# RWKV-7 recurrence on one core: the carry turned feature-major, head pairs issued in turn on row and column halves

## The chip, the core and the metric

One core of one Trainium2 chip runs the whole program. The metric is device time in microseconds. Before the change three runs gave 2215.01, 2234.22 and 2242.56 us, so the median is 2234.22 us. TensorE (PE) does the matrix products and writes its results to PSUM; VectorE (DVE), ScalarE (ACT) and GpSimd (POOL) do the element-wise work; SyncE (SP) issues loads.

## What is computed

For 4 batches and 8 heads of dimension 40, a state matrix is carried over 768 steps. Its output, rearranged to 4 x 768 x 320, then goes through a low-rank token mixer and a channel MLP:

```python
for t in range(S):
    y[:, :, t] = np.einsum('bhd,bhde->bhe', rt, state)
    Sa = np.einsum('bhde,bhe->bhd', state, at)
    state_decay = state * wt[:, :, None, :] - np.einsum('bhd,bhe->bhde', Sa, bt)
    state = state_decay + np.einsum('bhd,bhe->bhde', vt, kt)
...
h = xt @ U @ V
u = x + h.transpose(0, 2, 1)
ch = np.maximum(u @ w_ch1, 0.0) @ w_ch2
return (u + ch).astype(np.float32)
```

## The kernel before, in words

The program has two parts. Part 1 is the recurrence, in 24 units; a unit is one chunk of 128 steps of one batch, with its 8 heads as 4 pairs. Unit n is chunk n // 4 of batch n % 4, so the state of a batch is needed again four units later. Part 2 (the mixer and the MLP) follows and is not touched by the change.

A unit passes through three stages in three successive iterations of the loop at line 403. `prep` transposes the six inputs so that features lie on the partitions (head 0 of a pair from partition 0, head 1 from partition 64), forms the running product of w (`GT`, a scan) and its reciprocal (`ip`), scales A by the one and B and K by the other, and transposes K, B and the running product back (`tk`, `tb`, `tp`). `solve` runs once for each slot, that is for the four heads at one end of the pairs: it makes the scores `pf`, `pe` and `pc` from matmuls over 40 rows, and then inverts a 128 x 128 triangular matrix for each head by doubling blocks. Level 0 is a transpose; at each of the six further levels PE makes `px`, DVE turns it into `g`, PE makes `pt` and `pu`, ACT copies them to `tm` and `tt`, and POOL masks the next `fl` (lines 283 to 315). `carry` also runs once for each slot: it makes the right side `pr`, the solution `pX` with steps on the partitions and once more as `pXf` with features on the partitions, the new state `ps`, the product `pg`, the output `py` and the turned state `pS`. Its matmuls are mostly 40 columns wide.

A loop iteration takes `prep` of unit n, `solve` of unit n - 1 and `carry` of unit n - 2 in turn, one step of each at a time, until each is used up (line 412). A scheduler then fixes the order on each engine from this order, the dependencies and the free buffers. All PSUM tiles come from one pool of 8 banks. Each engine takes its own instructions strictly in that order.

The weights of part 2 arrive as 64-bit floats in 26 pieces (`raw`), one asked for in each iteration. DVE converts each with nine instructions at lines 132 to 144. The scheduler put all 26 in the first iterations, where they ended by 350 us.

In the profile's names `px<-tm,fl` is the instruction that writes `px` from `tm` and `fl`; 40*128 after MATMUL is rows x columns of the array in use. A float32 matmul of full precision stands in the records twice, a transpose once.

Of the kernel before, what the change touches and what calls it, by code (L numbers as in the profile page):

```python
# [12 lines left out]
outside, it redoes the recurrence step by step, which holds for any values.  # L13
"""
# [7 lines left out]
F32 = mybir.dt.float32  # L22
I32 = mybir.dt.int32
ALU = mybir.AluOpType
# [8 lines left out]
def kernel(  # L33
# [45 lines left out]
    # ML[l][t, s]: t and s in one block of 2n = 2^(l+1), s in its first half and t in its second.  # L79
# [19 lines left out]
    def weights(pool):  # L99
        """Loads part 2's weights, a piece at each step."""  # L100
# [47 lines left out]
    with ExitStack() as p1:  # L148
# [6 lines left out]
        S = st.tile([128, NB * NP, D], F32, name="S")  # L155
        ST = st.tile([128, NB * NP, D], F32, name="ST")
        # Per unit and partition: how many w are in range, and the other inputs' sums of squares.
# [34 lines left out]
        def prep(u):  # L192
            """Per unit of 8 heads: head pairs on the partitions (64 apart), steps on the free axis."""
# [51 lines left out]
            for key, t in (("k", fm["K"]), ("b", fm["B"]), ("p", gt)):  # L245
                p = psum(f"t{key}")
                for j in range(NP):
                    nc.tensor.transpose(out=p[:, j * L:(j + 1) * L], in_=t[:, j, 0:L], identity=ID[:])
                fm[key] = fmp.tile([128, NH, D], F32, name=f"t{key}", bufs=3)
                nc.scalar.activation(out=fm[key][:], func=ACTF.Copy,  # L250
                                     in_=p[:].rearrange("p (h e) -> p h e", e=DP)[:, :, 0:D])
                yield
# [5 lines left out]

        def solve(u, slot):
            """T, E and C of the 4 heads in one slot."""  # L260
            fm, q, lo = u.fm, u.q[slot], 64 * slot
            hi = lo + D

            def pairs(name, x, y):
                p = psum(name)
                for i in range(4):
                    nc.tensor.matmul(out=p[:, i * L:(i + 1) * L], lhsT=x[lo:hi, i, :],  # L267
                                     rhs=y[lo:hi, i, :], start=True, stop=True)
                return four(p)

            ft = qp.tile([128, 4, L], F32, name="ft")
            nc.scalar.activation(out=ft[:], in_=pairs("pf", fm["A"], fm["B"]), func=ACTF.Copy)
            yield
            q["E"] = qp.tile([128, 4, L], F32, name="E", bufs=3)
            nc.vector.tensor_tensor(out=q["E"][:], in0=pairs("pe", fm["K"], fm["A"]), in1=over4(MU),
                                    op=ALU.mult)
            yield
            q["C"] = qp.tile([128, 4, L], F32, name="C", bufs=3)
            nc.vector.tensor_tensor(out=q["C"][:], in0=pairs("pc", fm["V"], fm["R"]), in1=over4(MU),  # L279
                                    op=ALU.mult)  # L280
            yield
            tm = tt = None
            for l in range(NLEV):
                fl = qp.tile([128, 4, L], F32, name="fl", bufs=3)
# [9 lines left out]
                g = qp.tile([128, 4, L], F32, name="g", bufs=3)  # L294
# [23 lines left out]
        def carry(u, slot):  # L318
            """Outputs and the state at the chunk's end."""
            fm, q, lo = u.fm, u.q[slot], 64 * slot  # L320
            hi = lo + D
            first, last = u.c == 0, u.c == NCH - 1
            s0 = u.b * NP
            hs = [2 * i + slot for i in range(4)]
            s_, st_ = S[lo:hi, s0:s0 + NP, :], ST[lo:hi, s0:s0 + NP, :]

            def small(name, p0=0, p1=128):
                p = psum(name)
                return p[p0:p1, 0:4 * D].rearrange("p (i e) -> p i e", e=D)

            p = small("pr")
            for i in range(4):
                if not first:
                    nc.tensor.matmul(out=p[:, i, :], lhsT=fm["A"][lo:hi, i, :], rhs=st_[:, i, :],
                                     start=True, stop=False)
                nc.tensor.matmul(out=p[:, i, :], lhsT=q["E"][:, i, :], rhs=fm["v"][:, hs[i], 0:D],
                                 start=first, stop=True)
            rh = qp.tile([128, 4, D], F32, name="rh")
            nc.scalar.activation(out=rh[:], in_=p, func=ACTF.Copy)
            yield  # L340
            p = small("pX")
            for i in range(4):
                nc.tensor.matmul(out=p[:, i, :], lhsT=q["T"][:, i, :], rhs=rh[:, i, :],  # L343
                                 start=True, stop=True)
            nx = qp.tile([128, 4, D], F32, name="nx")
            nc.scalar.activation(out=nx[:], in_=p, func=ACTF.Copy, scale=-1.0)
            p = psum("pXf")
            for i in range(4):
                nc.tensor.matmul(out=p[lo:hi, i * L:(i + 1) * L], lhsT=rh[:, i, :], rhs=q["T"][:, i, :],
                                 start=True, stop=True)  # L350
            if u.xf is None:
                u.xf = qp.tile([128, 4, L], F32, name="xf", bufs=1)
            xf = u.xf
            nc.scalar.activation(out=xf[lo:hi], in_=four(p)[lo:hi], func=ACTF.Copy)
            yield
            if not last:
                p = small("ps", lo, hi)
                for i in range(4):
                    nc.tensor.matmul(out=p[:, i, :], lhsT=fm["k"][:, hs[i], :],
# [241 lines left out]
```

## Time and profile before

| | before |
|---|---|
| median of 3 runs | 2234.22 us (2215.01 to 2242.56) |
| span of the profiled execution | 2228.6 us |
| PE busy | 2188.2 us (98%) |
| DVE busy | 744.1 us (33%) |
| ACT busy | 488.5 us (22%) |
| POOL busy | 506.9 us (23%) |
| mean granted TensorE clock | 0.807 |

The profile covers one execution; it gives no other time for it than the span. Busy time is the time in which an engine had an instruction in work; for PE it says nothing on how full the array was. The granted clock is 1.0 where TensorE had its full 2.4 GHz and 0.5 where it had 1.2 GHz. The chain of work that ended last lies wholly on PE.

### The profile page before, as it was taken

Reading aid. Unit: us, or ns where it says so; the run is one execution under the profiler, and the core shown is the slowest. Engines: PE = TensorE matmul, PEld = TensorE weight load, DVE = VectorE, ACT = ScalarE, POOL = GpSimd, SP = SyncE. Lnnn points to the kernel's source line nnn. Section 1 sums busy time; section 2 is a strip of 40 time slices with the busy share of each in tenths; the row PEclk is TensorE's granted clock in tenths of the full one; section 3 lists DMA queues with packets and bytes.
Section 4 is the critical chain, followed back from the end, with each engine's and each line's share of the span. In section 5 each row is a group of like instructions: output and inputs, shape, how many; then the busy total and the mean of one; then the engine's idle time right before and its main releaser. Section 6 shows DMA issues by size and latency. Waiting matters only on the chain. (4 is left out here: it accounts for less than half of the span.)

```text
span 2228.6 us, 32787 instructions
## 1 busy us (share of the span) xinstructions
PE 2188.2 (98%) x13890; PEld 1921.7 (86%) x13890; DVE 744.1 (33%) x1439; ACT 488.5 (22%) x921; POOL 506.9 (23%) x453
## 2 busy tenths in 40 slices
PE   7999999999999999999999999999999999999999
PEld 6888898999999999999999999999999996565555
DVE  7666654323323323322333233233322121111111
ACT  2223221321321232132123213212321320000000
POOL 5333332322222232132223123222322320000000
PEclk8978876876886787688678678767866887999999
DMA  4111111000001001000100100000000000000000
GB/s 81 41 30 38 38 35 24 10 16 16 10 13 18 13 8 18 13 13 13 19 10 10 19 13 13 13 16 8 12 1 1 1 1 1 9 15 12 9 9 18
DMA packets 155286, 36.62 MB, mean 16 GB/s; under 512 B 150600, under 2 KB 153672, under 8 KB 155136
## 3 DMA queue, kind: packets, MB, share of 16 engines
q1 hardware_dynamic: 153216, 27.54, 6.7%
q0 software_dynamic: 1920, 6.95, 1.1%
q8 instruction: 111, 1.82, 0.3%
q14 instruction: 39, 0.32, 0.0%
HBM read 30.54 MB, written 3.93 MB: 15 GB/s over the span
## 5 line engine op out<-in xcount | busy, mean ns | idle before, releaser
L285 POOL TENSOR_TENSOR fl<-ft,ML 128x512 f32<-128x512 f32 x336 | 422.8, 1274 | 1220.7 <-PE px L291 541.2
L295 DVE TENSOR_TENSOR g<-ID,px 128x512 f32<-128x512 f32 x336 | 230.0, 687 | 494.4 <-PE px L291 487.2
L304 PE MATMUL pt<-g,tt 128*128 128x128 f32 x2304 | 311.7, 280 | 19.0 <-DVE g L295 16.7
L304 PEld LDWEIGHTS pt<-g,tt 128*128 128x128 f32 x2304 | 280.7, 193 | 27.7 <-DVE g L295 18.1
L311 PE MATMUL pu<-tt,g 128*128 128x128 f32 x1920 | 254.4, 276 | 0.0
L311 PEld LDWEIGHTS pu<-tt,g 128*128 128x128 f32 x1920 | 234.7, 193 | 0.0
L291 PE MATMUL px<-tm,fl 128*128 128x128 f32 x1920 | 234.0, 275 | 0.0
L291 PEld LDWEIGHTS px<-tm,fl 128*128 128x128 f32 x1920 | 224.0, 192 | 0.0
L307 ACT ACTIVATE tm<-pt 128x512 f32<-128x512 f32 x240 | 143.3, 597 | 218.4 <-PE pt L304 218.4
L314 ACT ACTIVATE tt<-pu 128x512 f32<-128x512 f32 x240 | 143.3, 597 | 74.9 <-PE pu L311 74.9
L543 PE MATMUL p<-uf,W 104*128 104x384 f32 (+1 forms) x480 | 156.4, 485 | 0.0
L543 PEld LDWEIGHTS p<-uf,W 104*128 104x128 f32 (+1 forms) x480 | 90.7, 189 | 63.3
L559 PE MATMUL p<-W,hid 128*128 128x320 f32 x480 | 136.1, 438 | 0.0
L559 PEld LDWEIGHTS p<-W,hid 128*128 128x128 f32 x480 | 89.0, 190 | 44.3 <-issue 10.5
L395 ACT ACTIVATE S<-pS 40x160 f32<-40x160 f32 x40 | 11.9, 299 | 499.7 <-PE pS L393 499.2
L279 DVE TENSOR_TENSOR C<-pc,MU 128x512 f32<-128x512 f32 x48 | 33.2, 692 | 239.0 <-PE pc L267 166.6
L381 PE MATMUL py<-tk,C 128*128 128x40 f32 x384 | 103.9, 364 | 0.0
L383 PE MATMUL py<-tb,ng 128*128 128x40 f32 x384 | 101.3, 358 | 0.0
L343 PEld LDWEIGHTS pX<-rh,tl 128*128 128x128 f32 x384 | 83.7, 321 | 13.8 <-issue 13.6
L548 ACT ACTIVATE hid<-p 128x384 f32<-128x384 f32 x40 | 19.6, 491 | 340.2 <-PE p L543 340.2
L371 PE MATMUL pg<-fR,xf 40*128 40x128 f32 x384 | 93.5, 431 | 0.0
L379 PE MATMUL py<-S,fR 40*128 40x40 f32 x320 | 91.9, 381 | 0.0
(138 smaller groups left out, 2832.4 us busy)
## 6 DMA issues: line engine op xcount, KB each, us to landing
nW<-in_w_dram SPq DMA_DIRECT2D x24, 160.0 KB, 2.6
nA<-in_a_dram SPq DMA_DIRECT2D x24, 160.0 KB, 2.6
nB<-in_b_dram SPq DMA_DIRECT2D x24, 160.0 KB, 2.6
nK<-in_k_dram SPq DMA_DIRECT2D x24, 160.0 KB, 2.5
nR<-in_r_dram SPq DMA_DIRECT2D x24, 160.0 KB, 2.6
nV<-in_v_dram SPq DMA_DIRECT2D x24, 160.0 KB, 2.5
out_dram<-o SPq DMA_DIRECT2D x24, 160.0 KB, 1.8
raw<-in_moe_w_ch_dram POOLq DMA_DIRECT2D x10, 320.0 KB, 3.2
```

The costliest lines, as they stand in the source:

```text
L285: nc.gpsimd.tensor_tensor(out=fl[:], in0=ft[:], in1=over4(ML[l]), op=ALU.mult)
L291: nc.tensor.matmul(out=p[:, i * L:(i + 1) * L], lhsT=fl[:, i, :], rhs=tm[:, i, :], start=True, stop=True)
L295: nc.vector.tensor_tensor(out=g[:], in0=over4(ID), in1=four(p), op=ALU.subtract)
L304: nc.tensor.matmul(out=p[:, i * L:(i + 1) * L], lhsT=tt[:, i, :], rhs=g[:, i, :], start=True, stop=True)
L307: nc.scalar.activation(out=tm[:], in_=four(p), func=ACTF.Copy)
L311: nc.tensor.matmul(out=p[:, i * L:(i + 1) * L], lhsT=g[:, i, :], rhs=tt[:, i, :], start=True, stop=True)
L314: nc.scalar.activation(out=tt[:], in_=four(p), func=ACTF.Copy)
L371: nc.tensor.matmul(out=p[:, i * L:(i + 1) * L], lhsT=xf[lo:hi, i, :], rhs=fm["R"][lo:hi, i, :], start=True, stop=True)
L381: nc.tensor.matmul(out=p[:, i, :], lhsT=q["C"][:, i, :], rhs=fm["k"][:, hs[i], :], start=first, stop=False)
L383: nc.tensor.matmul(out=p[:, i, :], lhsT=ng[:, i, :], rhs=fm["b"][:, hs[i], :], start=False, stop=True)
L543: nc.tensor.matmul(out=p[:, 0:GN], lhsT=W1[i][0:n, j * 128:(j + 1) * 128], rhs=uf[i][0:n, :], start=(i == 0), stop=(i == len(CT) - 1))
L559: nc.tensor.matmul(out=p[:, 0:DM], lhsT=hid[:, f, j * L:(j + 1) * L], rhs=W2[:, f, :], start=False, stop=(f == NJ - 1))
```

## The change

The scores of both slots are made together: for each of the three products the matmuls of the two heads of a pair are issued in turn, with head 0 on rows 0 to 63 of the array and head 1 on rows 64 to 127, into two PSUM tiles. The operands now span 64 rows with zeros beyond 40. The carry runs once for a unit, for all 8 heads, and keeps the right side, the solution and the output with features on the partitions. Its matmuls are 128 columns long (64 in the state products), and the two heads of a pair are issued in turn into column halves: head 0 writes partitions 0 to 63 and head 1 writes 64 to 127 of one PSUM tile. Where a product needs steps on the partitions, a transpose of four blocks (`flip`) turns it. In `prep` the two transposes of scaled K and B are replaced by one transpose of the reciprocal (`pi`) and two DVE products with the loaded K and B; the transpose of the running product is gone, since the output is scaled while its features lie on the partitions. The rings of `fl` and `g` have 2 buffers in place of 3. An iteration's steps are merged by a table of step counts (carry 8, prep 8, scores and inverse 17), so that a step of the carry comes after about every second step of the inverse.

```diff
+            p = psum("pi")
+            for j in range(NP):
+                nc.tensor.transpose(out=p[:, j * L:(j + 1) * L], in_=ip[:, j, :], identity=ID[:])
+            for key, t in (("k", "K"), ("b", "B")):
+                fm[key] = fmp.tile([128, NH, DP], F32, name=f"t{key}", bufs=3)
+                nc.vector.tensor_tensor(out=fm[key][:], in0=p[:].rearrange("p (h e) -> p h e", e=DP),
+                                        in1=u.nat[t][:], op=ALU.mult)
+            yield
...
+        def pairs(name, x, y):
+
+            out = [psum(f"{name}{s}") for s in range(2)]
+            for i in range(NP):
+                for s in range(2):
+                    nc.tensor.matmul(out=out[s][:, i * L:(i + 1) * L],
+                                     lhsT=x[DP * s:DP * (s + 1), i, :],
+                                     rhs=y[DP * s:DP * (s + 1), i, :], start=True, stop=True)
+            return [four(p) for p in out]
...
-                fl = qp.tile([128, 4, L], F32, name="fl", bufs=3)
+                fl = qp.tile([128, 4, L], F32, name="fl", bufs=2)
...
+        def columns(p, n, lhs, rhs, first, last):
+
+
+            for i in range(NP):
+                for s in range(2):
+                    nc.tensor.matmul(out=p[half(s), i * n:(i + 1) * n], lhsT=lhs(i, s), rhs=rhs(i, s),
+                                     start=first and i == 0, stop=last, skip_group_check=True)
+
+        def carry(u):
...
+            p = psum("pr")
+            columns(p, L, nat4(fm["v"]), score("E"), True, first)
+            if not first:
+                columns(p, L, feat(st_), feat(fm["A"]), False, True)
+            rf = qp.tile([128, NP, L], F32, name="rf", tag="xx", bufs=2)
+            nc.scalar.activation(out=rf[:], in_=four(p), func=ACTF.Copy)
+            yield
+            p = flip("prt", rf)
+            rh = qp.tile([128, NH, DP], F32, name="rh", tag="rn", bufs=1)
+            nc.vector.tensor_copy(rh[:].rearrange("p (i s) e -> p i (s e)", s=2), p)
+            yield
+            p = psum("pX")
+            columns(p, L, nat4(rh), score("T"), True, True)
...
+            for s, p in enumerate(pairs("pg", xf, fm["R"])):
+                t = qp.tile([128, NP, L], F32, name="ng")
+                nc.vector.tensor_tensor(out=t[:], in0=p, in1=over4(MUN), op=ALU.mult)
+                ng.append(t)
+            yield
+            py = psum("py")
+            columns(py, L, nat4(fm["k"]), score("C"), True, False)
+            columns(py, L, nat4(fm["b"]), lambda i, s: ng[s][:, i, :], False, first)
+            if not first:
+                columns(py, L, feat(s_), feat(fm["R"]), False, True)
...
+                columns(p, DP, nat4(fm["k"]), nat4(fm["v"]), True, False)
+                columns(p, DP, nat4(fm["b"]), nat4(nx), False, True)
...
+        def merged(*steps):
+
+            lists = [[g, 0, n] for g, n in steps]
+            while lists:
+                x = min(lists, key=lambda x: (x[1] + 0.5) / x[2])
+                if next(x[0], x) is x:
+                    lists.remove(x)
+                x[1] += 1
...
+            if n >= 2:
+                gens.append((carry(units[n - 2]), 8))
             if n < N:
-                gens.append(prep(units[n]))
+                gens.append((prep(units[n]), 8))
...
-            while gens:
-                gens = [g for g in gens if next(g, g) is not g]
+                gens.append((both(), 17))
+            merged(*gens)
```

The order on PE around the solution `pX` of one unit. Before, the pieces of the carry stand together, and one row of names holds one slot (`tl` is the finished inverse, `rh` the right side, `ps` the new state, `pg` and `py` the output's parts):

```order
L213 MATMUL pa<-ID,nA_140 128x128 x4
L267 MATMUL pe<-fA,fK 128x128 x8
L343 MATMUL pX<-rh,tl 128x40 x4
L349 MATMUL pXf<-tl,rh 40x128 x4
L343 MATMUL pX<-rh,tl 128x40 x4
L349 MATMUL pXf<-tl,rh 40x128 x4
L267 MATMUL pc<-fR,fV 128x128 x8
L359 MATMUL ps<-nV_132,tk 40x40
L361 MATMUL ps<-nx,tb 40x40
```

Now, from the scores to the second level of the inverse:

```order
L264 MATMUL pc_4889<-fR,fV 128x128
L264 MATMUL pc_4890<-fR,fV 128x128
L357 MATMUL prt<-ID,rf 128x128 x4
L213 MATMUL pa<-ID,nA_139 128x128 x4
L296 MATMUL px<-ID,fl 128x128 x8
L298 MATMUL px<-g,fl 128x128 x8
L333 MATMUL pX<-tl,rh 64x128 x8
L311 MATMUL pt<-g,tt 128x128 x4
L318 MATMUL pu<-tt,g 128x128 x4
L311 MATMUL pt<-g,tt 128x128 x4
L318 MATMUL pu<-tt,g 128x128 x4
L298 MATMUL px<-tm,fl 128x128 x8
```

The solution moved behind level 0 and the first `px` of level 1; `pXf` is gone, and `pg`, `py`, `ps` and `pS` now stand behind later levels, one at a time.

The order on DVE at the same place. Before, from the last `g` of one inverse on (`fA` is scaled A, `E` a masked score, `sink` a range test):

```order
L295 TENSOR_TENSOR g<-ID,px 128x512 x12
L224 SCALAR_TENSOR_TENSOR GT_153<-pw,zeros 128x128 x4
L197 TENSOR_SCALAR wc<-nW_147 128x8x40
L233 RECIPROCAL ip<-GT_153 128x512
L230 TENSOR_TENSOR fA<-pa,GT_153 128x512
L275 TENSOR_TENSOR E<-pe,MU 128x512 x2
L200 SCALAR_TENSOR_TENSOR sink,WOK<-nW_147,wc 128x320
```

Now:

```order
L302 TENSOR_TENSOR g<-ID,px 128x512 x4
L250 TENSOR_TENSOR tk<-pi,nK_127 128x512
L250 TENSOR_TENSOR tb<-pi,nB_143 128x512
L224 SCALAR_TENSOR_TENSOR GT_153<-pw,zeros 128x128 x4
L197 TENSOR_SCALAR wc<-nW_147 128x8x40
L233 RECIPROCAL ip<-GT_153 128x512
L278 TENSOR_TENSOR E<-pe_5405,MU 128x512
L278 TENSOR_TENSOR E<-pe_5406,MU 128x512
L282 TENSOR_TENSOR C<-pc_5419,MU 128x512
L369 COPY rh<-prt 128x512
L230 TENSOR_TENSOR fA<-pa,GT_153 128x512
L302 TENSOR_TENSOR g<-ID,px 128x512 x2
```

Before, the products of the carry (`sn`, `ng`) and the range tests also lay between the reciprocal and the next unit's first `g`, and on PE most of the carry. Now `wc`, the reciprocal and five products stand between the scan and the first `g`, and PE has only `pe`, `pc`, `prt`, `pa` and level 0 between `pw`, which the scan waits for, and the `px` of level 1, which waits for that `g`.

## Rows read from the trace of the kernel before

**Rows 1.** Stretches: us, then busy us (instructions) of PE, PEld, DVE, ACT, POOL; clock; DMA.

```profile
21.40:351.10 329.70, 310.73 (x2399) 294.92 (x2398) 215.94 (x452) 94.78 (x177) 115.45 (x105) 0.84 0.16 36
351.10:1684.60 1333.50, 1333.50 (x9134) 1242.98 (x9133) 427.87 (x800) 332.15 (x627) 340.39 (x272) 0.76 0.07 13
1684.60:1860.00 175.40, 174.74 (x1080) 161.93 (x1079) 37.57 (x57) 38.67 (x72) 39.99 (x32) 0.72 0.00 1
1860.00:2228.60 368.60, 362.08 (x1248) 214.94 (x1248) 49.44 (x92) 19.64 (x40) 0.00 (x0) 0.99 0.03 11
```

**Rows 2.** The same view: one regular unit, its inverse, most of its carry.

```profile
949.50:1028.00 78.50, 78.50 (x542) 73.17 (x541) 25.18 (x47) 19.58 (x37) 20.04 (x17) 0.76 0.08 14
949.50:987.00 37.50, 37.50 (x335) 36.38 (x334) 12.27 (x17) 17.48 (x32) 12.93 (x12) 1.00 0.03 5
987.00:1014.40 27.40, 27.40 (x142) 24.09 (x142) 9.70 (x25) 2.10 (x5) 4.64 (x5) 0.50 0.14 25
```

**Rows 3.** Timeline of PE in the inverse at 2.4 GHz: start us, us, instruction, records.

```profile
949.71 0.68 PE L393 MATMUL pS<-ID,ST 40*40 40x40 f32 x16
950.32 0.66 PE L213 MATMUL pV<-ID,nV 128*128 128x128 f32 x4
950.81 1.06 PE L304 MATMUL pt<-g,tt 128*128 128x128 f32 x8
951.70 1.06 PE L311 MATMUL pu<-tt,g 128*128 128x128 f32 x8
...
954.38 0.60 PE L213 MATMUL pR<-ID,nR 128*128 128x128 f32 x4
954.82 1.39 PE L291 MATMUL px<-tm,fl 128*128 128x128 f32 x11
```

**Rows 4.** Timeline of PE at 1.2 GHz where two scores of different row halves meet.

```profile
28.73 0.42 PE L267 MATMUL pe<-fA,fK 40*128 40x128 f32 x1
28.89 0.42 PE L267 MATMUL pc<-fR,fV 40*128 40x128 f32 x1
28.94 0.42 PE L267 MATMUL pe<-fA,fK 40*128 40x128 f32 x1
29.11 0.42 PE L267 MATMUL pc<-fR,fV 40*128 40x128 f32 x1
```

**Rows 5.** Groups by line: count, then busy us, mean ns of one, idle before.

```profile
L233 DVE RECIPROCAL ip<-GT 128x512 f32<-128x512 f32 x24 | 80.3, 3345 | 0.0
L224 DVE TENSOR_TENSOR_SCAN GT<-pw,zeros 128x128 f32<-128x128 f32 x96 | 32.8, 404 | 34.6 <-PE pw L213 34.6
L197 DVE TENSOR_SCALAR wc<-nW 128x320 f32<-128x320 f32 x24 | 9.8, 408 | 2.5 <-DMA nW<-in_w_dram 2.5
L275 DVE TENSOR_TENSOR E<-pe,MU 128x512 f32<-128x512 f32 x48 | 32.9, 689 | 41.8 <-PE pe L267 41.7
L295 DVE TENSOR_TENSOR g<-ID,px 128x512 f32<-128x512 f32 x336 | 230.0, 687 | 494.4 <-PE px L291 487.2 <-PE px L289 7.2
L285 POOL TENSOR_TENSOR fl<-ft,ML 128x512 f32<-128x512 f32 x336 | 422.8, 1274 | 1220.7 <-PE px L291 541.2 <-PE px L289 480.9 <-ACT ft L272 198.2
```

**Rows 6.** Stretches as in rows 1, where PE ran short of work early on.

```profile
103.00:106.40 3.40, 1.19 (x11) 0.95 (x10) 3.25 (x4) 0.44 (x1) 2.57 (x2) 1.00 0.29 48
106.40:109.80 3.40, 3.38 (x16) 3.38 (x17) 3.26 (x8) 0.60 (x1) 0.08 (x1) 0.50 0.02 5
109.80:113.20 3.40, 3.40 (x32) 3.40 (x32) 0.15 (x1) 2.12 (x4) 0.52 (x1) 1.00 0.28 78
```

**Rows 7.** Timeline of PE at 1.2 GHz, then (last row) at 2.4 GHz.

```profile
1011.11 1.11 PE L213 MATMUL pB<-ID,nB 128*128 128x128 f32 x4
1012.02 1.91 PE L289 MATMUL px<-ID,fl 128*128 128x128 f32 x8
...
1014.42 0.42 PE L381 MATMUL py<-tk,C 128*128 128x40 f32 x2
```

**Rows 8.** Waits: who for whom, total us, times, longest us.

```profile
DVE bits L132 <- DMA raw<-in_moe_w_ch_dram: 38.6, 21, 3.1
```

More of the change, by code (lines that the diff above doesn't have):

```diff
@@ L316, in solve @@
             q["T"] = tm
-        def carry(u, slot):
-            fm, q, lo = u.fm, u.q[slot], 64 * slot
-            hi = lo + D
-            first, last = u.c == 0, u.c == NCH - 1
[L323 to L327, printed above, removed]
-                p = psum(name)
[L329 to L339, printed above, removed]
-            yield
[L341 to L354, printed above, removed]
@@ L355, in carry @@
             yield
             if not last:
-                p = small("ps", lo, hi)
-                for i in range(4):
-                    nc.tensor.matmul(out=p[:, i, :], lhsT=fm["k"][:, hs[i], :],
-                                     rhs=fm["v"][:, hs[i], 0:D], start=True, stop=False)
-                    nc.tensor.matmul(out=p[:, i, :], lhsT=fm["b"][:, hs[i], :], rhs=nx[:, i, :],
-                                     start=False, stop=True)
-                pend = fm["g"][lo:hi, :, L:L + 1].to_broadcast([D, NP, D])
+                p = flip("pXt", xf)
@@ L364, in carry @@
                 if first:
-                    sn = p
+                    nc.vector.tensor_tensor(out=st_, in0=ps_, in1=pend, op=ALU.mult)
                 else:
-                    sn = qp.tile([128, 4, D], F32, name="sn")[lo:hi]
-                    nc.vector.tensor_tensor(out=sn, in0=p, in1=st_, op=ALU.add)
-            p = psum("pg")
-            for i in range(4):
-                nc.tensor.matmul(out=p[:, i * L:(i + 1) * L], lhsT=xf[lo:hi, i, :],
-                                 rhs=fm["R"][lo:hi, i, :], start=True, stop=True)
@@ L373, in carry @@
-            ng = qp.tile([128, 4, L], F32, name="ng")
-            nc.vector.tensor_tensor(out=ng[:], in0=four(p), in1=over4(MUN), op=ALU.mult)
-            yield
-            p = small("py")
-            for i in range(4):
-                if not first:
-                    nc.tensor.matmul(out=p[:, i, :], lhsT=fm["R"][lo:hi, i, :], rhs=s_[:, i, :],
-                                     start=True, stop=False)
-                nc.tensor.matmul(out=p[:, i, :], lhsT=q["C"][:, i, :], rhs=fm["k"][:, hs[i], :],
-                                 start=first, stop=False)
-                nc.tensor.matmul(out=p[:, i, :], lhsT=ng[:, i, :], rhs=fm["b"][:, hs[i], :],
-                                 start=False, stop=True)
@@ L385, in carry @@
-            x = XTM[:, u.b * NCH + u.c, :].rearrange("p (i s e) -> p i s e", s=2, e=D)[:, :, slot, :]
-            pt = fm["p"][:].rearrange("p (i s) e -> p i s e", s=2)[:, :, slot, :]
-            nc.vector.tensor_tensor(out=x, in0=p, in1=pt, op=ALU.mult)
-            if not last:
-                nc.vector.tensor_tensor(out=st_, in0=sn, in1=pend, op=ALU.mult)
-                yield
-                p = small("pS", lo, hi)
-                for i in range(4):
-                    nc.tensor.matmul(out=p[:, i, :], lhsT=st_[:, i, :], rhs=ID[lo:hi, lo:hi],
-                                     start=True, stop=True)
-                nc.scalar.activation(out=s_, in_=p, func=ACTF.Copy)
@@ L396, in carry @@
-            yield
+                    sn = qp.tile([128, NP, DP], F32, name="sn", tag="rn", bufs=1)
+                    nc.vector.tensor_tensor(out=sn[:], in0=ps_, in1=st_, op=ALU.add)
+                    nc.vector.tensor_tensor(out=st_, in0=sn[:], in1=pend, op=ALU.mult)
+                yield
+                p = psum("pS")
+                columns(p, DP, feat(st_), lambda i, s: ID[half(s), half(s)], True, True)
+                nc.scalar.activation(out=s_, func=ACTF.Copy,
+                                     in_=p[:, 0:NP * DP].rearrange("p (i e) -> p i e", e=DP))
@@ L404, with both @@
             gens = []
+            if n >= 2:
+                gens.append((carry(units[n - 2]), 8))
             if n < N:
-                gens.append(prep(units[n]))
+                gens.append((prep(units[n]), 8))
             if 1 <= n < N + 1:
-                gens += [solve(units[n - 1], 0), solve(units[n - 1], 1)]
-            if n >= 2:
-                gens += [carry(units[n - 2], 0), carry(units[n - 2], 1)]
-            while gens:
-                gens = [g for g in gens if next(g, g) is not g]
+                u = units[n - 1]
+                def both(u=u):
+                    yield from scores(u)
+                    g = [solve(u, 0), solve(u, 1)]
+                    while g:
+                        g = [x for x in g if next(x, x) is not x]
+                        yield
+                gens.append((both(), 17))
+            merged(*gens)
             next(wload, None)
```

82 lines of the change are left out of this document (52 added, 30 removed).

## The prediction

> **What bounds the kernel now.** I read first the stretches of the whole program, then those of one unit, then the timeline of TensorE (PE) inside it, and last the groups by line for what the other engines cost. Over the 17 units from 351 us on, PE is busy for all of 1333.5 us, 78.4 us a unit, at a mean clock of 0.76 [rows 1]. In one unit DVE is busy for 25.2 of 78.5 us, ACT for 19.6, POOL for 20.0 [rows 2]. So PE sets the pace, and the question is what it does. The inverse runs 37.5 us at 2.4 GHz; in the 27.4 us of carry and scores behind it the clock is 0.50, that is 1.2 GHz, though PE shows no gap [rows 2]. A unit is thus about half dense work at full clock and half small work at half clock. In the five units before 351 us PE lacks work for 19 us in all and DVE is busy for 216 of 330 us [rows 1], since the weights are converted there; DVE also waited 38.6 us for their pieces [rows 8]. Part 2 takes 368.6 us [rows 1] and stays.
>
> **The sum for PE, per unit, at 2.4 GHz.**
> - Inverse, unchanged: a group of four matmuls takes 0.89 us from start to start [rows 3]. 34 groups are 30.3 us. The 8 transposes of level 0, at 0.11 each (four in 0.44 [rows 3]), are 0.9 us.
> - Transposes: 28 in `prep` (36 before) and 12 in the carry (none before): 40 x 0.11 = 4.4 us.
> - Row halves: 24 scores and 8 of `pg`. Where a score of one half met one of the other, both streams kept their own rate: `pe` starts at 28.73 and 28.94, `pc` at 28.89 and 29.11, a record each 0.21 us in each stream at 1.2 GHz [rows 4]. A matmul is two records, so two halves together make two matmuls in 0.43 us, or one each 0.107 us at 2.4 GHz. 32 x 0.107 = 3.4 us. Before, heads of one half followed each other in fours, and so overlapped only at the seams.
> - Halves in both directions (state times A, state times R): the diagonal `pS` matmuls took 16 records in 0.61 us with a change of mode in it [rows 3], less than one by one at the same length. 16 x 0.107 = 1.7 us, and `pS` again 0.6.
> - Column halves over all 128 rows: 32 matmuls 128 columns long, and 16 of `ps` half as long. No row of before shows these. They are bounded by 0.107 (as the row halves) and 0.22 us (one after another, a quarter of 0.89 [rows 3]). I take 0.107, because both kinds of halves that rows show overlap. 3.4 + 0.9 = 4.3 us; by the upper bound 8.8.
> - Changes of mode: the new order has 17 a unit. The transposes behind `pS` took 0.49 us where four alone take 0.44, and the entry is part of the 0.61 [rows 3]. I take 0.1 us for each, 1.7 us.
>
> Sum: 30.3 + 0.9 + 4.4 + 3.4 + 1.7 + 0.6 + 4.3 + 1.7 = 47.3 us if the clock stays at 2.4 GHz and nothing waits. A rule of the Trainium skill speaks against the change here: "TensorEngine Tiling (Array Packing)", Key Properties, says that changing the tiling mode drains TensorE. By rows that drain is the 0.1 us above, and even 0.3 for each would leave 50.7.
>
> **What PE will wait for.** DVE takes its work in order. At the seam of two units it holds, once `pw` is there: four scans (4 x 0.40), `wc` (0.41), the reciprocal (3.35), two `E`, one `C`, `rh`, `fA` and the first `g` (6 x 0.69) [rows 5], 9.5 us in all. The products `tk` and `tb` stand before the scans and are done while `pw` is awaited. From the last `g` of a unit PE needs 1.0 us for the last `pt`, 0.9 for `pyt` and `pi`, 1.0 for `pf`, 2.0 for `pr` and 0.5 for `pw`, so `g` comes at 5.4 + 9.5 = 14.9 us. Behind `pw` PE has `pe` and `pc` (1.9), `prt` and `pa` (0.9) and level 0 (0.9), and so is through at 9.1 us. It then waits 5 to 6 us for `g`; I take 5.5. Before, the reciprocal was hidden by the long `pr`, `pX` and `pXf` at 1.2 GHz; that cover is what the change removes.
>
> Other DVE work is covered: the range tests, `ng`, `yf`, `sn` and the new state stand where PE has a group of `pt` and `pu` (3.6 us) to do first. POOL's next `fl` costs 2 x 1.27 us [rows 5] from the end of a `px`, and that buffer is wanted 4.5 us later, so two buffers suffice in place of three. ACT copies about as much as before, and its 20 us a unit [rows 2] stay far below 56. SP's loads of K and B now wait until `tk` and `tb` have read the old ones, a whole unit ahead of their use.
>
> The wait costs clock too. Where PE was busy for only 1.19 of 3.4 us, the clock was 0.50 in the next stretch, and 16 records were done there where the one behind, at 1.00, took 32 [rows 6]. I expect one such drop a unit with 4 us of PE work left in it: 2 us. Handovers as they now are around each `g` add 1 us. So a unit is 47.3 + 5.5 + 2 + 1 = 55.8; I say 56 us.
>
> **The sum for the program.** From 351 to 1685 us: 17 x (78.4 - 56) = 381 us less. The last steps, 175.4 us [rows 1]: a unit without state (54), an inverse with carry and no `prep` (44), a carry alone, eight handovers of some 2.5 us (20), so 118, or 57 less. The five early units, 330 us: DVE's 216 us grow by some 2 us a unit and by three more conversions at 4 us (now 25 in this stretch), and its waits for pieces add up to 38.6 us. That makes 240 to 280 us on DVE in order with PE's 250. I take 295, or 35 less. Part 2: nothing. 2228.6 - 381 - 57 - 35 = 1755.6 us of span. The median of the runs lies 5.6 us above the span, so **1761 us**; the handovers at the start that I can't price make me say 1765.
>
> **The rivals.**
> - Column halves run one after another: 4.5 us a unit, over 23 units 104 us, **1870 us**. Against it: the row halves; for it: no row shows it. "TensorE: Matmul & The Clock Gate", Part 3 of the Trainium skill, says that weights load beside running matmuls only where their row group differs, which column halves don't do. The trace disagrees for full-size matmuls: loads of 0.19 us each would not fit otherwise into 0.89 us for four. Chance 0.20.
> - The change doesn't do what it says: no halves overlap at all. Then row halves and diagonals cost 5.1 us more as well: 9.6 a unit, **1985 us**. Rows 4 speak against it. Chance 0.06.
> - The clock falls earlier, because transposes don't hold it up; the stretch before the wait is mostly transposes (28 of them, 3.1 us, from `pyt` to level 0). These and the first dense matmuls would run at 1.2 GHz: 3 us more a unit, 1835 us; and if the wait grew to 10 us by the longer DVE queue, **1930 us**. Part 4 of the same page of the Trainium skill says that transposes don't engage the full clock. The trace disagrees: at 1.2 GHz twelve transposes, `pB` and `px`, were followed by a `py` at 2.4 GHz [rows 7]. Chance 0.08.
> - No wait at the seam, because DVE is ahead: 5.5 + 2 us less a unit, **1600 us**. Against it is the order on DVE. Chance 0.05.
> - Slower: the small pieces, spread among the inverse, keep the clock at 1.2 GHz all through, where before the inverse had 37.5 us at 2.4 GHz in one piece. 47.3 us become 94.6, with DVE's wait then hidden: 16 us more a unit, some 23 x 16 = 370, **2600 us**. It decides once 45 us of a unit lie at 1.2 GHz, since 56 + 45/2 is 78.5. Against it: what was slow before were 40-column and 40-row pieces, and the new pieces fill rows and are 128 long. Chance 0.04.
>
> **How the numbers follow.** My forecast, 1765 us, has 0.57 with a range of its own of 1700 to 1830: 53 to 59 us a unit. The range of 1690 to 1920 adds the column halves and the milder clock case, and leaves out the other ends. Within 2% of 2234 (2190 to 2279, about what a measurement of this kernel can tell from no change) is hardly any case: 0.02. Faster 0.94, slower 0.04.
>
> **What would show it.** In the profile after: `px` and `pt` groups at 0.89 us; `pe` and `pc` 16 records in 0.9 us and the 16 matmuls of `py` in column halves in 1.7 us (3.5 if one after another); PE idle for 5 to 6 us a unit before the `px` of level 1, released by DVE's `g`, with the reciprocal in front of it; the clock at 0.93 or so in part 1. A unit of over 60 us, a clock below 0.85, or waits of PE elsewhere would make the prediction wrong.

## The result and the profile after

The changed kernel takes **1778.4 us** (median of 4 runs, 1776.1 to 1780.1) against 2227.3 us (4 runs, 2215.0 to 2242.6): a ratio of 0.799, interval 0.795 to 0.804. The prediction said 1765, range 1690 to 1920.

The changed kernel's page, cut to its span, the engines' busy time, and one group by line:

```profile
span 1778.4 us, 32076 instructions
PE 1590.9 (89%) x13586; PEld 1371.8 (77%) x13586; DVE 822.1 (46%) x1451; ACT 445.2 (25%) x777; POOL 507.5 (29%) x453
...
L298 PE MATMUL px<-g,fl 128*128 128x128 f32 x384 | 86.4, 416 | 143.9 <-DVE g L302 142.3
```

PE is no longer busy all the time, and most of its idle time in part 1 (142.3 of some 171 us) stands in front of one line: the `px` of level 1, for DVE's `g`. The stretches that answer to [rows 1] (five early units, 17 units, last steps, part 2; columns as there):

```profile
20.10:337.80 317.70, 245.99 (x2375) 231.04 (x2373) 252.04 (x469) 87.42 (x152) 116.30 (x107) 0.91 0.17 39
337.80:1299.60 961.80, 875.39 (x8927) 825.37 (x8925) 468.22 (x802) 302.83 (x525) 341.58 (x274) 0.95 0.10 18
1299.60:1412.70 113.10, 100.17 (x1001) 93.57 (x1000) 39.69 (x59) 33.01 (x57) 38.69 (x32) 0.96 0.01 1
1412.70:1778.40 365.70, 361.97 (x1248) 215.13 (x1248) 49.44 (x92) 19.61 (x40) 0.00 (x0) 0.99 0.03 11
```

A unit now takes 961.8 / 17 = 56.6 us where it took 78.4. One unit, from its `pw` to the next, and then the same unit in three pieces (same columns; it answers to [rows 2]):

```profile
904.40:961.30 56.90, 51.82 (x531) 48.84 (x529) 27.61 (x47) 17.88 (x31) 20.07 (x17) 0.94 0.11 19
904.40:912.20 7.80, 4.56 (x54) 4.01 (x52) 7.09 (x10) 0.60 (x1) 6.32 (x6) 1.00 0.23 40
912.20:919.00 6.80, 4.96 (x28) 4.77 (x30) 5.58 (x11) 0.00 (x0) 2.33 (x2) 0.50 0.14 24
919.00:961.30 42.30, 42.30 (x453) 40.06 (x449) 14.95 (x28) 17.29 (x30) 11.42 (x10) 1.00 0.08 15
```

Of 56.9 us, 5.1 are idle and 6.8 lie at 1.2 GHz, from the last 1.8 us of the idle time on; the rest is at 2.4 GHz, where before the carry's 27.4 us were at half that. The timeline of PE at this seam (start us, us, instruction, records; in brackets idle time before, and who ended it):

```profile
902.37 1.09 PE L333 MATMUL pr<-E,nV 128*64 128x128 f32 x16
903.40 1.09 PE L333 MATMUL pr<-fA,ST 64*64 64x128 f32 x16
904.42 0.66 PE L213 MATMUL pw<-ID,wc 128*128 128x128 f32 x4
905.00 1.16 PE L264 MATMUL pe<-fA,fK 64*128 64x128 f32 x16
906.00 1.06 PE L264 MATMUL pc<-fR,fV 64*128 64x128 f32 x16
...
907.92 1.04 PE L296 MATMUL px<-ID,fl 128*128 128x128 f32 x8
914.04 3.75 PE L298 MATMUL px<-g,fl 128*128 128x128 f32 x16 [5.08 <-DVE g L302]
```

And DVE at the same time:

```profile
905.11 1.37 DVE L224 TENSOR_TENSOR_SCAN GT<-pw,zeros 128x128 f32<-128x128 f32 x4 [2.44 <-PE pw L213]
906.40 0.71 DVE L197 TENSOR_SCALAR wc<-nW 128x320 f32<-128x320 f32 x1
907.03 3.34 DVE L233 RECIPROCAL ip<-GT 128x512 f32<-128x512 f32 x1
910.29 1.22 DVE L278 TENSOR_TENSOR E<-pe,MU 128x512 f32<-128x512 f32 x2
911.43 0.67 DVE L282 TENSOR_TENSOR C<-pc,MU 128x512 f32<-128x512 f32 x1
912.03 0.67 DVE L369 COPY rh<-prt 128x512 f32<-128x512 f32 x1
912.63 0.68 DVE L230 TENSOR_TENSOR fA<-pa,GT 128x512 f32<-128x512 f32 x1
913.22 1.27 DVE L302 TENSOR_TENSOR g<-ID,px 128x512 f32<-128x512 f32 x2
```

PE's level 0 was done by 909; `g` of slot 0 starts at 913.22, 8.80 us behind `pw`, because DVE works through its queue without a gap. That is the wait the prediction named, with the reciprocal in it. Column halves: the 16 records of `pr<-E,nV` take 1.03 us from start to start, one change of mode included.

### The profile page after: what moved, and what is told of

Read it like the earlier page. It is cut to its first block, busy times and chain, and to the rows that moved or that the text cites. A ratio compares the mean times of both kernels' runs of the same rounds, so it can differ in the third digit from the quotient of the medians.

```text
span 1778.4 us, 32076 instructions
## 1 busy us (share of the span) xinstructions
PE 1590.9 (89%) x13586; PEld 1371.8 (77%) x13586; DVE 822.1 (46%) x1451; ACT 445.2 (25%) x777; POOL 507.5 (29%) x453
## 5 line engine op out<-in xcount | busy, mean ns | idle before, releaser
L311 PE MATMUL pt<-g,tt 128*128 128x128 f32 x2304 | 318.8, 283 | 20.1 <-DVE g L302 19.3
L298 PE MATMUL px<-g,fl 128*128 128x128 f32 x384 | 86.4, 416 | 143.9 <-DVE g L302 142.3
L298 PEld LDWEIGHTS px<-g,fl 128*128 128x128 f32 x384 | 80.9, 321 | 149.1 <-issue 147.1
L374 ACT ACTIVATE xf<-pX 128x512 f32<-128x512 f32 x24 | 14.3, 597 | 341.8 <-PE pX L333 258.3
L583 DVE TENSOR_SCALAR hid<-p 128x384 f32<-128x384 f32 x40 | 22.3, 558 | 133.2 <-PE p L580 133.2
L233 DVE RECIPROCAL ip<-GT 128x512 f32<-128x512 f32 x24 | 80.2, 3341 | 0.0
L599 DVE TENSOR_TENSOR o<-p,XTM 128x320 f32<-128x320 f32 x24 | 11.8, 492 | 134.8 <-PE p L596 134.8
```

Source lines behind the costliest of these rows:

```text
L233: nc.vector.reciprocal(out=ip[:], in_=gt[:, :, 1:L + 1])
L298: nc.tensor.matmul(out=p[:, i * L:(i + 1) * L], lhsT=fl[:, i, :], rhs=tm[:, i, :], start=True, stop=True)
L311: nc.tensor.matmul(out=p[:, i * L:(i + 1) * L], lhsT=tt[:, i, :], rhs=g[:, i, :], start=True, stop=True)
L583: nc.vector.tensor_scalar_max(hid[:, j, :], p[:, 0:GN], 0.0)
```

## The experiments

Eleven kernels. `col_serial`, `row_serial`, `spread_alone` and `no_spread`, the first, second, fourth and fifth below, have 2 runs each, the others 4. Times are medians, and the ratio is to the kernel before, run beside it. Where no ratio stands, those runs gave no interval.

### Which halves pay

**Column halves not in turn.** In `columns`, the two loops change places, so that all heads of one half come before the other half:

```diff
-            for i in range(NP):
-                for s in range(2):
+            for s in range(2):
+                for i in range(NP):
```

> The changed kernel with the column halves issued one head after the other (four matmuls of head 0, then four of head 1) in place of in turn; nothing else differs. Theory (halves in turn overlap, halves in blocks overlap only at the seam): each block of eight 128-column matmuls grows from about 1.0 us to 1.7 to 1.8 us, four such blocks and two of half length a unit, 4.0 us a unit, 23 units: 1778 + 92 = 1870 us. Rival (the array overlaps them whatever their order, or did not overlap them before either): 1770 to 1785 us.

Measured: 1850.0 us, ratio 0.830 (0.824 to 0.837), so 71.6 us more than the change. Two groups in this kernel's timeline of PE, beside 1.03 and 1.02 us from start to start in the changed kernel:

```profile
883.68 1.58 PE L333 MATMUL pr<-E,nV 128*64 128x128 f32 x16
885.19 1.58 PE L333 MATMUL pr<-fA,ST 64*64 64x128 f32 x16
```

Each takes 1.51 us, half a microsecond more. So column halves and diagonals overlap when issued in turn, which no row of before showed, and this is worth 3.5 us a unit (its 17 units took 1021.7 us in place of 961.8; 0.25 us a unit of it is a longer wait for `g`). It is less than the 4.5 of the rival, since the end of one half still overlaps the start of the other: the records there are 0.05 us apart, where in the rest of the group they are 0.11.

**Row halves not in turn.** The same edit in `pairs` (`pf`, `pe`, `pc`, `pg`).

> The changed kernel with the row halves of the scores and of pg issued one head after the other; nothing else differs. Theory: pf, pe, pc and pg grow by 0.8 us each, but pe and pc stand before the 5 us wait of TensorE at the seam of two units and are swallowed by it; pf is ahead of pw, on which the scan waits, and counts, and so does pg: 1.6 us a unit, 1778 + 37 = 1815 us, with the wait 1.6 us shorter. Rival (the wait is not set by DVE's chain behind pw): all four count, 3.2 us a unit, 1850 us. Rival (no overlap by rows): 1778 us.

Measured: 1771.9 us, ratio 0.795 (0.789 to 0.802): no slower than the change, and under every time that was expected. `pf` and `pg` cost 0.55 us more each, and `pe` with `pc` took 2.7 instead of 2.0 us, but the wait that follows shrank. The same `px` as above, in this kernel (its `pw` starts at 837.51), and DVE beside it:

```profile
845.66 1.27 DVE L302 TENSOR_TENSOR g<-ID,px 128x512 f32<-128x512 f32 x2
846.49 3.75 PE L298 MATMUL px<-g,fl 128*128 128x128 f32 x16 [3.68 <-DVE g L302]
846.86 0.32 DVE L197 TENSOR_SCALAR wc<-nW 128x320 f32<-128x320 f32 x1
```

PE idles 3.68 us in place of 5.08, for two reasons. 0.75 us is the longer `pe` and `pc`: what PE saves ahead of a wait for DVE it spends waiting. The other 0.65 is a change that the edit did not ask for: the scheduler put the clamp `wc`, which took 0.71 us ahead of `g`, behind it, so that `g` starts 8.15 us behind `pw` instead of 8.80. This hides more than half of what `pf` and `pg` cost, so the time does not show that row halves are worth nothing. The 17 units took 967.2 us in place of 961.8, and the five early ones 305.5 in place of 317.7; in the early ones PE's waits for `g` at line 298 fell from 51.3 to 26.2 us, and the section on the prediction says what the clamp has to do with it.

**The row halves alone, in the kernel before.** The scores of both slots are issued in turn ahead of the inverse; the carry keeps its old shapes and order.

```diff
+        def scores(u):
+            fm = u.fm
+            for s, p in enumerate(pairs("pf", fm["A"], fm["B"])):
...
-                gens += [solve(units[n - 1], 0), solve(units[n - 1], 1)]
+                gens.append(both())
```

> The kernel before with only the three score matrices changed: both slots' row halves issued in turn, sixteen to a group, ahead of the inverse; the carry keeps its shapes and its order. Theory of the row halves: 24 matmuls fewer in sequence, 3.4 us a unit at 2.4 GHz, of which the changed kernel showed nothing since its TensorE waits for VectorE there; in the kernel before half of that stretch runs at 1.2 GHz, so 3 to 6 us a unit would show if TensorE is the bound there, 22 x 3 = 66 to 22 x 6 = 132 us less: 2100 to 2165. Rival, from the run with row halves serial: the wait for VectorE at the head of a unit swallows it here too: 2215 to 2235. Rival: the scores of both slots ahead of the inverse delay level 0 of slot 0 and lengthen the wait: 2240 to 2290.

Measured: 2028.4 us, ratio 0.918 (0.908 to 0.929), far below what was expected. The 17 units of this kernel:

```profile
301.30:1492.00 1190.70, 1190.70 (x9134) 1115.06 (x9133) 423.35 (x800) 330.89 (x627) 339.09 (x272) 0.84 0.08 14
```

PE is busy all through, and a unit takes 70.0 us where it took 78.4. Nearly all of that is the clock, 0.84 in place of 0.76. An estimate from these rows: 1333.5 us at 0.76 [rows 1] are some 1013 us of work at 2.4 GHz, and 1190.7 us at 0.84 some 1000. So of the 143 us that the 17 units gained, the halves' own time is no more than some 13. Whether the halves or the new order of the scores raised the clock, this run doesn't separate; the next one shows that an order alone can.

### What the spreading does

**Old shapes, new spreading.** The kernel before with its carry's steps spread by the change's rule.

> The kernel before with its carry spread among the inverse's steps by the same kind of table (carry 5 steps of both slots, prep 10, inverse 17), all shapes as they were. Theory (shapes pay): the 40-column and 40-row pieces need 60 us a unit even at 2.4 GHz and still drop the clock round pr and py: 66 to 72 us a unit, 1960 to 2090 us. Rival (spreading pays by the clock): 62 us or less a unit and a clock over 0.92: under 1880 us. Rival (spreading does nothing): 2200 to 2240 us.

Measured: 2059.6 us, ratio 0.925 (0.918 to 0.931). Its 17 units:

```profile
312.70:1528.00 1215.30, 1214.99 (x9133) 1139.16 (x9132) 459.70 (x800) 332.07 (x628) 344.70 (x272) 0.85 0.08 14
```

The old shapes run faster spread out, with PE still busy throughout. By the same estimate the work is 1033 us at 2.4 GHz, no less than the 1013 before: the gain is the clock's.

**New shapes, old order.** The steps of `prep`, scores and inverse, and carry are again taken one each in turn.

```diff
-            merged(*gens)
+            gens = [g for g, _ in gens[1:] + gens[:1]] if n >= 2 else [g for g, _ in gens]
+            while gens:
+                gens = [g for g in gens if next(g, g) is not g]
```

> The changed kernel with the old order of steps: one step of prep, of scores and inverse, and of the carry in turn until each is used up, so that the carry stands together at the unit's start. Theory (the new shapes pay, not their spreading): TensorE's work is the same 47 us, the small work now stands where DVE does its scan and reciprocal, so the wait shrinks: 1740 to 1800 us, clock at 0.93 or more. Rival (the spreading among the inverse keeps the clock up): the carry drops the clock to 1.2 GHz again for some 15 us a unit and the time is over 1850 us.

Measured: **1682.2 us**, ratio 0.755 (0.750 to 0.760). The spreading, good for the old shapes, costs the new ones 96 us (61.7 of them in the 17 units, 30.3 in the early ones). Their clock is 0.98 without it. PE at the one wait of a unit in this kernel:

```profile
952.00 1.32 PE L333 MATMUL pX<-tl,rh 128*64 128x128 f32 x16 [2.77 <-DVE rh L369]
```

Taken in turn, more of the carry and of `prep` stands around level 0: PE waits 2.8 us for `rh`, behind the same reciprocal on DVE, and the level 1 `px` not at all. The spread order leaves PE with 4.0 us of work behind `pw`, while DVE's `g` starts only 8.8 us behind the start of `pw`.

### What the wait is

**Reciprocal replaced by a copy.** (`nc.vector.tensor_copy` in its place.)

> The changed kernel with VectorE's reciprocal of the running product (3345 ns in [rows 5]) replaced by a copy of the same 128x512 (computation left out: keys are then scaled by the product, not by its inverse). TensorE's wait at the seam is 5.2 us a unit in the changed kernel's trace, for VectorE's g behind scans, wc, reciprocal, E, C, rh and fA. Theory: the wait is that chain, so it shortens by the 2.7 us that a copy of this shape saves (3.35 less about 0.65, the price of rh's copy), 22 units x 2.7 = 59 us, to 1719 us; if the stretch at 1.2 GHz that follows the wait (3.4 or 6.8 us a unit) shrinks with it, up to 1 to 1.5 us more a unit, to 1690. Rival: what g waits for is something else (a free PSUM bank, POOL's masks, the order in which carry's copies come), and the reciprocal stands beside it: 1770 to 1780. Rival: TensorE is at its own bound but for the clock, no gain in time, the wait moves to a later g: 1760 to 1780.

Measured: 1763.2 us, ratio 0.799 (0.790 to 0.807): 15 us less than the change, with the same ratio, which looked like the rival. The timeline of DVE, POOL and PE in this kernel, whose `pw` starts at 891.75, shows why it is not:

```profile
892.99 2.58 POOL L307 TENSOR_TENSOR tt<-ID,fl 128x512 f32<-128x512 f32 x2
894.36 1.49 DVE L233 COPY ip<-GT 128x512 f32<-128x512 f32 x1
896.00 2.73 POOL L292 TENSOR_TENSOR fl<-ft,ML 128x512 f32<-128x512 f32 x2 [0.43 <-PE px L296]
896.97 0.64 DVE L200 SCALAR_TENSOR_TENSOR sink<-nW,wc 128x320 f32<-128x320 f32 x1
898.15 0.93 DVE L207 SCALAR_TENSOR_TENSOR sink<-nA 128x320 f32<-128x320 f32 x1
...
900.22 1.27 DVE L302 TENSOR_TENSOR g<-ID,px 128x512 f32<-128x512 f32 x2
901.03 3.75 PE L298 MATMUL px<-g,fl 128*128 128x128 f32 x16 [4.74 <-DVE g L302]
901.41 0.48 DVE L207 SCALAR_TENSOR_TENSOR sink<-nB 128x320 f32<-128x320 f32 x1
```

The copy saves 1.85 us, and two range tests (`sink`) that stood elsewhere moved into the gap, as the scheduler ordered DVE anew. `g` comes 8.47 us behind `pw` instead of 8.80. The experiment shortened an instruction and not the queue.

**`rh` on ScalarE, in the version with the old order.**

> The version with the new shapes and the old order (steps of prep, inverse and carry in turn), and rh's copy moved from VectorE to ScalarE, which was idle for 6.8 us there. In that version TensorE idles 2.8 us a unit before pX for rh, which stands on VectorE behind wc, the reciprocal, fA, two sinks and both E; then 3.4 us run at 1.2 GHz, which cost 1.7 us. Theory: with rh on ScalarE pX starts right behind pc, the wait of 2.8 us goes and the stretch at 1.2 GHz with it, 22 units x 2.8 = 62 to 22 x 4.5 = 99 us less than 1682: 1583 to 1620; if the next wait (level 1's px for g behind VectorE's same chain) takes part of it, 1630 to 1660. Rival: pX also waits for the inverse's last factor or a PSUM bank, no gain: 1675 to 1690.

Measured: 1698.4 us, ratio 0.769 (0.760 to 0.778), where without it the ratio was 0.755 (0.750 to 0.760). It is no faster, and the theory of this edit fell. The waits of PE in this kernel (total us, times, longest):

```profile
PE pg L264 <- DVE C L282: 26.2, 18, 2.4
PE px L298 <- DVE g L302: 25.7, 20, 6.2
```

They take the place of 60.5 us of `pX` for `rh`. `pX` starts at once, and PE then stops for the next two things from the same DVE queue. The new waits add up to a little less (51.9 us), but the mean clock fell from 0.979 to 0.970. One late item was moved, the lateness stayed.

**The queue itself shortened.** The whole computation is kept; only DVE's order changes, by an edge from a `g` to the instruction that shall follow it. `late_recip2` is the change with this edit, `no_spread_late2` the version with the old order with it (and `V`, `R` transposed ahead of the reciprocal). The range tests follow later `g` in the same way:

```diff
+        def behind(u, k, lev):
+            v = units[u.n - k] if u.n >= k else None
+            return nullcontext() if v is None or lev not in v.at else tc.issue_after(v.at[lev])
...
+            with behind(u, 2, 4):
                 nc.vector.tensor_scalar(out=wc[:, :, 0:D], ...
...
+            with behind(u, 1, 1):
                 nc.vector.reciprocal(out=ip[:], in_=gt[:, :, 1:L + 1])
```

> The changed kernel, whole computation, with VectorE's order alone changed: the reciprocal stands behind g of level 1 (it stood between the scans and E), the clamp wc behind g of level 4 of the unit ahead, the range tests (sink) behind g of levels 2 to 4. The run with the reciprocal replaced by a copy gained 15 us only, because two range tests moved into the 1.9 us that it freed: g still came 8.5 us behind pw, against 8.8. Theory: TensorE's wait at the seam is the length of VectorE's queue there, whatever stands in it. Now scans 1.37, E 1.22, C, rh, fA 0.6 each and g 0.64 are left, so the first g ends some 6 us behind pw instead of 9.4: 3.3 us of the 5.2 go, 22 units x 3.3 = 73 us, to 1705; with the 1.2 GHz stretch behind the wait gone too (3.4 us, 1.7 lost, in 22 units) down to 1668. Rival: the wait only moves, to g of level 2 behind the reciprocal, or to fB and fK: 1750 to 1790. Rival: something else than VectorE's queue releases g: 1765 to 1785.

> The version with the new shapes and the old order of steps (1682 us), with the same relief of VectorE at the seam: reciprocal behind g of level 1, V's and R's transposes ahead of it, clamp and range tests behind later g. Moving rh's copy to ScalarE there gained nothing (1698): TensorE then waited as long for C and for g, all behind the same queue. Theory: the queue is the price, so taking the reciprocal, wc and two range tests (6.2 us together) out of it ends the 2.9 us wait at pX and the 1.2 GHz stretch with it: 22 units x 2.9 to 4.6 = 64 to 101 us less, 1580 to 1620. Rival: the wait goes to level 2's px, behind reciprocal, C, yf, sn, fB and ST (7 us) on VectorE: 1640 to 1690. Rival: TensorE's own work is the bound: no gain, 1675 to 1690.

Measured: **1659.1 us**, ratio 0.748 (0.743 to 0.753), and **1616.0 us**, ratio 0.729 (0.724 to 0.734). In `late_recip2`, first the 17 units, then the `px` of level 1 (its `pw` starts at 830.45):

```profile
321.80:1184.10 862.30, 841.30 (x8927) 791.53 (x8925) 490.25 (x798) 303.00 (x525) 339.89 (x274) 1.00 0.11 20
```

```profile
835.40 1.27 DVE L310 TENSOR_TENSOR g<-ID,px 128x512 f32<-128x512 f32 x2
836.22 2.18 PE L306 MATMUL px<-g,fl 128*128 128x128 f32 x16 [1.24 <-DVE g L310]
```

| kernel | `g` behind `pw` | PE idle | a unit | clock in the 17 units |
|---|---|---|---|---|
| changed | 8.80 us | 5.08 us | 56.6 us | 0.95 |
| reciprocal a copy | 8.47 | 4.74 | 56.2 | 0.95 |
| reciprocal, clamp and range tests late | 4.95 | 1.24 | 50.7 | 1.00 |

PE's wait follows the start of `g` (3.85 us earlier, 3.84 less idle), and the stretch at 1.2 GHz behind it is gone, worth another 2.0 us. That is the theory shown, with no arithmetic left out. The rival, that the wait would turn up at level 2, is out: PE is busy for 841 of 862 us. One unit of `no_spread_late2`, whole:

```profile
745.20:794.90 49.70, 49.51 (x530) 46.58 (x528) 27.84 (x47) 17.90 (x31) 19.98 (x16) 1.00 0.12 21
```

PE is busy for 49.5 of 49.7 us at 2.4 GHz: its own work is the bound again, and this is the sum that the prediction put at 47.3.

### The early units

**No conversion on VectorE.**

> The changed kernel without the nine VectorE instructions that turn each piece of part 2's weights from 64 to 32 bits; the transfers stay and GpSimd fills the weight's tile with a constant (part 2's weights are left out of the computation). In the changed kernel the first five units take 318 us where 17 later ones take 56.6 each; 25 of 26 pieces are converted in those five. Theory: VectorE's conversions are what makes the early units long, so they come to about 57 each: 318 - 285 = 33 us less, 1745 us, perhaps to 1735 with the stretches at 1.2 GHz that follow the waits. Rival: the early units are long for the transfers of the weights beside the loads on the same memory, or for cold buffers: 1770 to 1780.

Measured: 1741.4 us, ratio 0.788 (0.780 to 0.797), 37 us less, all of it in the first five units of this kernel:

```profile
21.40:302.40 281.00, 244.21 (x2374) 231.26 (x2372) 140.99 (x235) 87.43 (x152) 115.29 (x108) 0.91 0.19 42
302.40:1263.40 961.00, 874.48 (x8926) 824.52 (x8924) 468.27 (x802) 302.98 (x525) 341.39 (x273) 0.95 0.10 18
```

DVE has 111 us less to do there, and the five units take 281.0 us in place of 317.7; PE's own time is the same. The transfers were kept, so they alone are not the cause. About half of the gain lies in PE's waits ahead of the `px` of level 1: 32.5 us (25.8 for `g`, 6.7 for POOL's `fl`) in place of 51.3. At three of these seams no conversion stood in DVE's queue, but with the conversions went a delay of the clamp, which took 0.5 us there where it had taken 6.1; the next section comes back to it.

**The best version: one piece a unit.** `no_spread_late2`, with each piece's conversion behind the `g` of level 3 of its iteration:

```diff
-            next(wload, None)
+            g = units[min(max(n - 1, 0), N - 1)].at
+            with tc.issue_after(g[3]) if 3 in g else nullcontext():
+                next(wload, None)
```

> The 1616 us version with the conversions of part 2's weights held to one piece a unit, each behind g of level 3, where 25 of 26 were converted in the first units. In that version the first five units take 279.5 us and 17 later ones 49.8 each, with TensorE busy for 49.5 of them at 2.4 GHz: 279.5 - 249 = 30 us are to be had. Theory (the early units are long for VectorE's conversions, as the run without them showed): the first five fall to about 52 each, the later ones lengthen by no more than 0.5 each since VectorE is busy for 28 of 50 us: 1585 to 1600. Rival: one conversion (some 5 us of VectorE) between g of levels 3 and 4 makes TensorE wait in every unit, 1 to 2 us x 22: 1605 to 1635. Rival: part 2 waits for its last pieces, now converted behind the last units: 1600 to 1620.

Measured: **1584.8 us** (1584.4 to 1585.1; the kernel before beside it 2192 to 2248), 31 us under `no_spread_late2` and 194 under the change. Early units and later ones of this kernel:

```profile
17.60:256.50 238.90, 232.27 (x2343) 219.59 (x2342) 164.26 (x284) 86.06 (x149) 103.93 (x86) 0.99 0.15 28
256.50:1104.50 848.00, 842.66 (x8926) 791.00 (x8924) 554.87 (x951) 303.50 (x525) 349.71 (x289) 1.00 0.13 26
```

The five come to 47.8 us each, the later ones to 49.9: the conversion costs 0.2 us a unit where DVE has room for it. The last steps, with the last pieces now among them, take 113.8 us in place of 108.9.

## Why the prediction was right

- **The bound.** "PE sets the pace" held, and the place of the new wait, its releaser and the reciprocal in it were as said. The table above shows that the wait is the length of DVE's queue.
- **The unit, 56 us.** Measured 56.6. Its terms: the wait was put at 5.5 and was 5.1. The clock was put at 2 us; PE is busy 51.5 us a unit (875.39 over 17) where the same work takes 49.5 at 2.4 GHz (841.30 over 17 in `late_recip2`), so 2.0. PE's work with the handovers was put at 48.3 and is 49.5. By the starts in `late_recip2` the inverse takes some 32.8 us, put at 31.2 and 1 for the handovers, and the rest 16.8, put at 16.1. In the inverse the first group of `pt` behind most `px` takes 0.99 us from start to start and the next group 0.89; why, no run says.
- **Column halves, 0.107 us.** Close: eight matmuls took 1.03 us with a change of mode and 0.92 without (`py<-C,tk`), and with the loops changed round 1.51. The rival at 1870 is out for the change: it priced no overlap at all at 4.5 us a unit, and halves in blocks, which overlap a little, cost 3.5. The rival's page, the Trainium skill's "TensorE: Matmul & The Clock Gate", Part 3, lets weights load beside running matmuls only where the row group differs. The trace disagrees for column halves as well as for full-size matmuls: the loads for `pr<-E,nV` are busy for 0.85 of its 1.09 us, and both heads use all 128 rows. One reason given for 0.107 was weak. The `pS` row does not show that diagonals overlap: 0.61 us for eight are 0.076 each, or 0.064 without the 0.1 for the change of mode, and before, `ps` took 0.13 us each one after another at 1.2 GHz (starts at 1004.96, 1005.09 and 1005.22), or 0.067 at 2.4. That diagonals overlap was first shown by `col_serial`, 1.02 us against 1.51.
- **Row halves.** Put at 3.4 us, all of it counted. What `pe` and `pc` save by them, 0.75 us against blocks, buys nothing, since they stand ahead of the wait. What `pf` and `pg` save, 0.55 us each, does count; the 1771.9 us without it hide that, since DVE's queue lost the clamp in the same run. The sum was right because the wait was counted from PE's shortened time. It is PE's time plus the wait that counts there, and that is set by DVE.
- **The spreading.** Not priced as a step of its own, and this was the gap in the prediction. It was taken as the order in which the wait arises, and what the other order would give was not asked: 96 us less. With DVE's queue shortened it still costs 43 (1659.1 to 1616.0), 22 of them in the early units (301.7 to 279.5) and 18 in the 17 later ones.
- **The early units, 295 us.** The term that was off: 317.7. I set DVE's 240 to 280 us beside PE's 250 and let them overlap. DVE has 252 and PE 246, as said, but at each seam PE waits for DVE, twice as long as in the later units. The waits of PE in the changed kernel from 20 to 338 us (total us, times, longest), and DVE and POOL at one of these seams:

```profile
PE px L298 <- DVE g L302: 51.3, 5, 11.3
```

```profile
273.16 2.50 POOL L292 TENSOR_TENSOR fl<-ft,ML 128x512 f32<-128x512 f32 x2
274.59 6.13 DVE L197 TENSOR_SCALAR wc<-nW 128x320 f32<-128x320 f32 x1
275.62 2.48 POOL L307 TENSOR_TENSOR tt<-ID,fl 128x512 f32<-128x512 f32 x2
278.06 2.47 POOL L292 TENSOR_TENSOR fl<-ft,ML 128x512 f32<-128x512 f32 x2
```

  DVE's order from the scans to `g` is here the same as in the later units. What differs is the clamp `wc`, which the prediction put at 0.41 us: it takes 6.13 us at three of the five seams and 5.48 at a fourth, and 0.71 in the later units, and it ends when POOL's work does. The excess over 0.71 is 21 us in all, nearly the whole miss. Where `wc` stands behind the first `g` (row halves not in turn), PE waits 3.68 us at the same three seams. The early units as a whole are 22.7 of the 22.8 us by which the span (1778.4) exceeds the sum (1755.6); the units' 10 us more cancel against the last steps (113.1 for 118), part 2 and the start. The 5.6 us added for the median did not come: median and span are both 1778.4.
- **The clock.** It did not fall through the stretch of transposes: it is 1.00 up to 912.2, 3.2 us into the idle time. The rival that the transposes don't hold it up, and the one that the small pieces keep it down, are out for this kernel; with the wait down to 1.2 us it is 1.00 throughout the 17 units.

## What to carry to other kernels

A shape that packs TensorE is worth what it saves only where TensorE ends the stretch; ahead of a wait for another engine it is worth nothing, so price the other engine's queue at each seam before the shapes. When a wait is behind an in-order queue, shorten the queue by moving what nobody there needs, and look at the new order afterwards: a shorter instruction lets others in, an edit elsewhere can move an instruction out, and moving one waiting consumer away exposes the next. So compare the orders before a time that did not change is read as an edit without effect. An order that suited long, slow pieces has to be priced again when the pieces get short.

## What the runs showed of the hardware

Some DVE instructions between SBUF tiles took longer while POOL worked. In the run with the copy, `ip<-GT` took 0.41 to 0.42 us in the five executions that met no POOL work, and 1.49 in the rows above; a `sink` took 0.93 at 898.15 with POOL at work, and one of the same shape 0.48 at 901.41 with POOL idle. In the changed kernel `wc` took 0.30 and 0.31 us in the two units where POOL was idle and 6.13 in the rows above. The reciprocal, also from SBUF to SBUF, did not: all 24 took 3.34 to 3.35 us, 19 of them beside POOL's work. By the Trainium skill's "SBUF — State Buffer", section "SBUF: two separate sides", some VectorE instructions (those with two SBUF inputs, or in a mode that uses both ports) and GpSimd lock a pair of ports against each other. The rows fit it, but no run here took POOL's work away, so that it is the cause was not tested; nor do the rows say why `wc` was let in sooner in the later units.

Small operands alone did not keep the clock low: units whose scores and carry are halves of 64 rows or columns ran at 1.00 from end to end once PE's idle time was 1.2 us in place of 5.1.
